# Attention blocks in pairs, q times state in four quadrants of TensorE, and y in two PSUM banks, in a gated linear attention with a squared-ReLU FFN

## The chip, the cores and the metric

The kernel runs on one core of one Trainium2 chip. The metric is the device time of one execution in microseconds (us), the median of several executions.

## The reference

Per batch and head (4 x 8, sequence 768, head size 48) a 48 x 48 state decays and is read at each token, and the result, heads side by side, goes through a feed-forward network with squared ReLU. All of it is float32 on TensorE; the two weight matrices come as float64 words and are converted on the chip.

```python
for t in range(S):
    state = alpha[:, :, t, :, None] * state + einsum('bhd,bhe->bhde', k[:, :, t], v[:, :, t])
    y[:, :, t] = einsum('bhd,bhde->bhe', q[:, :, t], state)
x = y.transpose(0, 2, 1, 3).reshape(3072, 384)
out = np.maximum(x @ w_in, 0) ** 2 @ w_out        # w_in 384 x 2048, w_out 2048 x 384
```

## The kernel before, in words

**Blocks and groups.** The sequence is cut in 6 chunks of 128 tokens. A block `n` is one chunk `c = n // 4` of one batch; there are 24. Four blocks, the four batches of a chunk, make a group of 512 tokens, and the FFN works on one group at a time while the attention of the next group is interleaved with it. The heads of a block are handled as `NP = 4` pairs `p`, with `e` = 0 or 1 for the even and the odd head of a pair; the even head lives in partitions 0 to 47, the odd one in 64 to 111.

**Steps of one attention block**, each a small function (lines of the kernel before): `aT`, `qT`, `kT` (L211) transpose alpha, q and k on TensorE; `ln` (L220, ScalarE) takes the logarithm, `sn` (L225, VectorE) the running sum in time, `eb` and `ei` (L234, L238, ScalarE) its exponential and the inverse; `mq` and `mk` (L248, VectorE) scale q and k by them into `qs` and `ks`; `sc` (L261, TensorE) forms the scores of the eight heads with the even heads on the lower and the odd ones on the upper half of the rows; `am` (L269, VectorE) copies the causal half of the scores to `am_t`, one copy for even and one for odd heads; `kr` (L279) turns `ks` back and `kc` (L284, ScalarE) copies it; `kv` (L290) multiplies it by v for the state; `sm` and `st` (L305, L356, VectorE) update the state `s_t`; `y` forms the output in PSUM, and `ev` (L345, ScalarE) copies it in 12 pieces to `xT`, the transposed input of the FFN.

**The product y** has two parts that accumulate in one PSUM bank. The first (L318) is q times state: the states of the two heads of a pair lie on the diagonal of a 128 x 128 tile that is zero elsewhere, so that one matmul does two heads, four in a block; all 128 rows and columns of TensorE are used. The second (L325) is scores times v: eight matmuls of 128 rows and 48 or 64 columns, alternating between the lower and the upper half of the columns.

**PSUM** has two pools of four banks: `ps_att` for the attention (and for every second tile of the first FFN product in groups 1 to 5), and `ps_ffn`. Tiles are given out round robin.

**Stages in time.** First the attention of blocks 0 to 3, in an order that is written out by hand. Then group 0: 16 units `ffn_in` (L425) and 32 units `ffn_out` (L498), spread over 16 slots; each slot also has one stage of attention of the next four blocks and one call of `next_weights`, which starts the load of one weight chunk, finishes the conversion of another (`convert_second`, L147 to L154, VectorE) and begins a third (`convert_first`, L130 to L140, VectorE and ScalarE). Then groups 1 to 5, each with a first product `ffn_in_pair` (L461), which has no attention beside it, and a second one, 28 units `ffn_product` (L532) of four matmuls. Beside those units the attention of the next group runs: `PLAN` (L628) gives for each step the unit at which it is issued, counted from the start of its block, and `BEGIN` (L632) the four starts, 0, 6, 12 and 18. Every unit and step issues in this one order on all engines, so each engine's queue is in the order of the plan. `sum_x` (L373, VectorE) makes sums of `xT` for the following first product. `combine` at L373 also makes sums of the hidden tiles after units 5 to 16.

**Loads** go over the SP queue; `load(n + 1)` is issued at `aT` of block `n`. The inputs a, q and k have two buffers each, v has three; `qs` and `ks` have one.

Of the kernel before, what the change touches and what calls it, by code (L numbers as in the profile page):

```python
# [15 lines left out]
GB = 4  # L16
# [7 lines left out]
def kernel(  # L24
# [46 lines left out]
    def kept(name, n, shape):  # L71
        return [consts.tile(shape, FP32, name=f"{name}{i}") for i in range(n)]

    NIN = 2
    NV = 3
    tiles = {x: kept(f"{x}_in", NIN, [128, H, 64]) for x in "aqk"}
# [1 line left out]
        for x, value in (("a", 1.0), ("q", 0.0), ("k", 0.0)):  # L78
            nc.gpsimd.memset(tiles[x][i][:, :, D:64], value)
    tiles["v"] = kept("v_in", NV, [128, H * D])  # L80
    s_t = kept("s", B, [128, NP, 128])
    for t in s_t:
        nc.gpsimd.memset(t, 0.0)

# [33 lines left out]
    half = {}  # L118
# [54 lines left out]
    am_t = kept("am", NAM, [128, 2, NP, 128])  # L173
# [120 lines left out]

    def state(n, e):
        rows = slice(64 * e, 64 * e + D)
        return rows, s_t[n % B][rows, :, 80 * e : 80 * e + D]

    def sm(n):
        if n // B in range(1, NCH - 1):  # L300
# [6 lines left out]
                )  # L307
            blk[n]["kv"] = t

    def y(n):  # L310
        v_in = tiles["v"][n % NV]

        per = NP // 2 if n == GB - 1 else NP
        ys = blk[n]["y"] = [bank(n, "y", (per, C)) for _ in range(NP // per)]

        if n // B:
            for p in range(NP):
                nc.tensor.matmul(  # L318
                    out=ys[p // per][:, p % per, :],
                    lhsT=s_t[n % B][:, p, :], rhs=blk[n]["qs"][:, p, :],  # L320
                    start=(p % per == 0), stop=False, skip_group_check=True,
                )
        for p in range(NP):
            for e in range(2):
                nc.tensor.matmul(  # L325
                    out=ys[p // per][64 * e : 64 * e + D + G * e, p % per, :],
                    lhsT=v_in[:, (2 * p + e) * D - G * e : (2 * p + e + 1) * D],
                    rhs=am_t[n % NAM][:, e, p, :],
                    start=(n // B == 0 and p % per == 0), stop=True, skip_group_check=True,
                )  # L330

    def ev(n):
        g, t = divmod(n, GB)
        if t == 0:
            xT[g] = x_pool.tile([128, KM, GB * C], FP32, tag="xT", name="xT")
        ys = blk[n].pop("y")
        per = NP // len(ys)

        for p in range(NP):
            copy = nc.vector.tensor_copy if p >= per else nc.scalar.copy  # L340
            for r, f, end in ((64, 2 * p * D + 32, 2 * (p + 1) * D), (0, 2 * p * D, (2 * p + 1) * D)):
                while f < end:
                    kk, to = divmod(f, 128)
                    m = min(end - f, *(RUN[i % 128] for i in (r, to)))
                    copy(  # L345
                        out=xT[g][to : to + m, kk, t * C : (t + 1) * C],
                        in_=ys[p // per][r : r + m, p % per, :],
                    )
                    r, f = r + m, f + m

    def st(n):
        if n // B < NCH - 1:
# [16 lines left out]
    HT, HM, NR2 = GB * C // 2, DM // 2, NJ // 4  # L369
# [144 lines left out]
    PRODUCTS = (("1", 0), ("5", 3), ("6", 1), ("7", 2), ("2", 0), ("4", 2), ("3", 3))  # L514
# [64 lines left out]
    steps = {f.__name__: f for stage in stages for f in stage}  # L579
# [14 lines left out]

    def attention(i):
        n, k = divmod(i, len(stages))
        if n < NBLK:
            for f in stages[k]:  # L600
                f(n)
            if k == 0 and n + 1 < NBLK:
                load(n + 1)

    NS = GB * len(stages)
    NG = NBLK // GB
    units = [(KM * GB * C, ffn_in, (0, j)) for j in range(NJ)]

    units += [(NJ // NW * DM, ffn_out, (0, t, i)) for i in range(NW) for t in range(GB)]
    total = sum(c for c, _, _ in units)  # L610
    done = 0
    attention(NS)
    for slot in range(NS):
        if slot < NS - 1:
            attention(NS + slot + 1)
        next_weights()
        if 0 <= slot - (NS - 3) < NR2:
            sum_w_in(slot - (NS - 3))
        if slot == NS - 1:
            sum_x(1)  # L620
        while units and done * NS < total * (slot + 1):
            c, f, args = units.pop(0)
            f(*args)
            done += c
    sum_w_in(NR2 - 1)
    NU = len(PRODUCTS) * NR2

    PLAN = (  # L628
        (0, (aT, ln, sn, eb, ei)), (2, (qT, mq, kT, mk)), (4.5, (kr, kc)), (5, (sc, am)),
        (5.5, (kv,)), (6.5, (sm, y, ev, st)),  # L630
    )
    BEGIN = (0, 6, 12, 18)  # L632
    for g in range(1, NG):

        for j in range(NJ // 2 + 1):
            for i, step in enumerate("ABacCDd"):
                if j - step.islower() in range(NJ // 2):
                    ffn_in_pair(g, j - step.islower(), step)
                if g == 1 and j < NJ // 2 and i in (1, 4):
                    sum_w_out(2 * j + i // 4)  # L640
        todo = [
            (begin + at, f, NS // len(stages) * (g + 1) + t)
            for t, begin in enumerate(BEGIN) for at, fs in PLAN for f in fs
        ]
        todo = sorted(todo, key=lambda x: x[0]) + [(NU - 3, sum_x, g + 1)]
        for u in range(NU):
            while g + 1 < NG and todo and todo[0][0] <= u:
                _, f, n = todo.pop(0)
                f(n)
                if f == aT and n + 1 < NBLK:  # L650
                    load(n + 1)
            ffn_product(g, *divmod(u, NR2))


# [28 lines left out]
```

## Time and profile before

| what | us |
|---|---|
| median of 3 runs | 616.08 |
| lowest and highest of them | 614.52, 617.27 |
| the profiled execution | 615.03 |
| its span in the profile | 613.2 |
| TensorE busy (PE) | 599.4 |
| VectorE busy (DVE) | 372.3 |
| ScalarE busy (ACT) | 245.6 |

The span runs from the first to the last instruction of the program; 1.83 us of the profiled execution lie around it. PE are the matmuls and PEld the loads of their stationary operand, which overlap them. A float32 matmul appears as two records, so a unit of four matmuls shows as x8; transposes have one record each. In a row of groups, `out<-in` names the tiles, then come the shapes, the count, busy time and the mean of one in ns, and the idle time of the engine ahead of them with what ended it. In a row of the timeline the first number is the start in us from the beginning of the span, the second the length to the end of the last instruction of the row; matmuls are pipelined, so the difference of two starts tells what a row took, not its length.

### The profile page before, as it was taken

The numbers are of one execution on the slowest core, as the hardware profiler recorded it, in microseconds if no ns is written. First come the engines' busy times: TensorE is split into PE (matmuls) and PEld (weight loads), VectorE is DVE, ScalarE is ACT, GpSimd is POOL, SyncE is SP. The second block draws the span as 40 slices with busy tenths as digits, with TensorE's granted clock in tenths as the row PEclk, the third lists the DMA queues.
The fourth block names the chain that finished last, engine by engine and source line by source line (L and its number), as shares of the span: only waits on it lengthen the run. The fifth ranks groups of instructions, "written<-read, shape, count | busy, mean of one in ns | idle before, by whom it ended". The sixth has DMA issues, their size and how long they took to land.

```text
span 613.2 us, 9325 instructions
## 1 busy us (share of the span) xinstructions
PE 599.4 (98%) x3684; PEld 516.1 (84%) x3684; DVE 372.3 (61%) x685; ACT 245.6 (40%) x613; POOL 3.8 (1%) x18
## 2 busy tenths in 40 slices
PE   7889999999999999999999999999999999999997
PEld 4755456667889999889999988999988999988997
DVE  6776858787775754565664466574456564356440
ACT  3859785532333443234333333343233244323200
POOL 2000000000000000000000000000000000000000
PEclk8979999999999999999999999999999999999999
DMA  9978375404003320403330400332130220000001
GB/s 151 255 180 188 105 152 168 91 1 104 0 1 66 52 40 27 78 1 53 53 52 13 90 2 5 61 56 36 53 52 0 53 52 2 29 25 0 1 1 51
DMA packets 108715, 36.77 MB, mean 60 GB/s; under 512 B 100480, under 2 KB 103552, under 8 KB 108672
## 3 DMA queue, kind: packets, MB, share of 16 engines
q1 hardware_dynamic: 108672, 36.18, 28.8%
q8 instruction: 29, 0.48, 0.4%
q14 instruction: 14, 0.11, 0.1%
HBM read 31.46 MB, written 4.72 MB: 59 GB/s over the span
## 4 chain that ended last, share of the span: by engine, by line
PE 87%; ACT 5%; DVE 5%; issue 1%; DMA 1%; SPq 0%; DVEq 0%
PE h L461 31%; PE o L532 31%; PE o L498 7%; PE sc L261 4%; PE y L325 3%; PE y L318 3%; PE kv L290 2%; ACT xT L345 2%; PE aT L211 1%; PE kr L279 1%; PE qT L211 1%; PE kT L211 1%; PE h L425 1%; DVE power L147 1%; ACT hid L431 1%
## 5 line engine op out<-in xcount | busy, mean ns | idle before, releaser
L461 PE MATMUL h<-xT,w_in 128*128 128x256 f32 x480 | 124.0, 379 | 0.0
L461 PEld LDWEIGHTS h<-xT,w_in 128*128 128x128 f32 x480 | 91.1, 190 | 12.4
L345 ACT COPY xT<-y 32x128 f32<-32x128 f32 (+3 forms) x282 | 72.8, 258 | 38.9 <-PE y L325 33.4
L532 PE MATMUL o<-w_out,hid 128*128 128x192 f32 x480 | 84.9, 329 | 0.0
L532 PEld LDWEIGHTS o<-w_out,hid 128*128 128x128 f32 x480 | 77.3, 190 | 1.9 <-issue 1.4
L474 DVE TENSOR_TENSOR hid<-h,u 128x256 f32<-128x256 f32 x120 | 50.9, 424 | 28.8 <-PE h L461 25.0
L479 ACT ACTIVATE hid<-hid 128x256 f32<-128x256 f32 x40 | 16.7, 417 | 114.6 <-DVE hid L474 114.6
L269 DVE COPY_PREDICATED am<-causal,sc 128x512 f32<-128x512 uint32 x48 | 32.3, 728 | 41.8 <-PE sc L261 41.8
L474 DVE TENSOR_TENSOR u<-h,u 128x256 f32<-128x256 f32 x80 | 33.9, 423 | 33.6 <-PE h L461 21.2
L225 DVE TENSOR_TENSOR_SCAN la<-again,la 128x512 f32<-128x512 f32 x24 | 29.4, 1223 | 33.3 <-ACT la L220 33.3
L461 PE MATMUL h<-s3x,ws 128*128 128x256 f32 x160 | 47.6, 379 | 0.0
L425 PE MATMUL h<-xT,w_in 128*128 128x512 f32 x96 | 43.5, 603 | 1.5 <-DVE w_in L154 1.5
L498 PE MATMUL o<-w_out,hid 128*128 128x384 f32 x128 | 42.8, 489 | 0.4 <-DVE w_out L154 0.4
L532 PE MATMUL o<-t,s 128*128 128x192 f32 x240 | 42.4, 328 | 0.0
L461 PE MATMUL h<-s3x,w_in 128*128 128x256 f32 x160 | 41.1, 379 | 0.0
L532 PEld LDWEIGHTS o<-t,s 128*128 128x128 f32 x240 | 38.9, 190 | 0.5
L498 PEld LDWEIGHTS o<-w_out,hid 128*128 128x128 f32 x128 | 23.7, 190 | 16.2 <-ACT r L430 0.6
L425 PEld LDWEIGHTS h<-xT,w_in 128*128 128x128 f32 x96 | 18.0, 194 | 21.6 <-issue 20.4
L220 ACT ACTIVATE la<-aT 128x512 f32<-128x512 f32 x24 | 14.2, 593 | 52.4 <-PE aT L211 52.3
L461 PEld LDWEIGHTS h<-s3x,w_in 128*128 128x128 f32 x160 | 30.4, 190 | 4.1
L461 PEld LDWEIGHTS h<-s3x,ws 128*128 128x128 f32 x160 | 30.4, 190 | 4.1
L261 PEld LDWEIGHTS sc<-qs,ks 48*128 48x128 f32 x384 | 23.3, 187 | 6.4 <-issue 3.3
(93 smaller groups left out, 849.6 us busy)
## 6 DMA issues: line engine op xcount, KB each, us to landing
raw<-in_moe_w_in_dram SPq DMA_DIRECT2D x8, 768.0 KB, 6.4
raw<-in_moe_w_out_dram SPq DMA_DIRECT2D x8, 768.0 KB, 4.3
a_in<-in_alpha_dram SPq DMA_DIRECT2D x24, 192.0 KB, 3.3
q_in<-in_q_dram SPq DMA_DIRECT2D x24, 192.0 KB, 4.0
k_in<-in_k_dram SPq DMA_DIRECT2D x24, 192.0 KB, 4.5
v_in<-in_v_dram SPq DMA_DIRECT2D x24, 192.0 KB, 4.3
out_dram<-osb SPq DMA_DIRECT2D x24, 192.0 KB, 2.0
```

The lines of the kernel that those rows point to most:

```text
L211: nc.tensor.transpose(out=ps[:, p, :], in_=rows[:, 128 * p : 128 * (p + 1)], identity=ident)
L225: nc.vector.tensor_tensor_scan(out=la.rearrange("a p t -> a (p t)"), data0=again.rearrange("a p t -> a (p t)"), data1=la.rearrange("a p t ...
L261: nc.tensor.matmul(out=ps[e][:, p, :], lhsT=blk[n]["ks"][rows, p, :], rhs=blk[n]["qs"][rows, p, :], start=True, stop=True,)
L269: nc.vector.copy_predicated(out=am_t[n % NAM][:, e], mask=causal.bitcast(U32).unsqueeze(1).to_broadcast([128, NP, C]), data=ps,)
L318: nc.tensor.matmul(out=ys[p // per][:, p % per, :], lhsT=s_t[n % B][:, p, :], rhs=blk[n]["qs"][:, p, :], start=(p % per == 0), stop=False, ...
L325: nc.tensor.matmul(out=ys[p // per][64 * e : 64 * e + D + G * e, p % per, :], lhsT=v_in[:, (2 * p + e) * D - G * e : (2 * p + e + 1) * D], ...
L345: copy(out=xT[g][to : to + m, kk, t * C : (t + 1) * C], in_=ys[p // per][r : r + m, p % per, :],)
L425: nc.tensor.matmul(out=ps, lhsT=w[:, kk, c0 : c0 + 128], rhs=xT[g][:, kk, :], start=(kk == 0), stop=(kk == KM - 1),)
L461: nc.tensor.matmul(out=ps, lhsT=a, rhs=b, start=(step.isupper() and i == 0), stop=(i == len(pairs) - 1), skip_group_check=True,)
L474: nc.vector.tensor_tensor(out=o, in0=ps, in1=z, op=ALU.add)
L498: nc.tensor.matmul(out=acc[t][:, 0:DM], lhsT=hid[i][:, j, t * C : (t + 1) * C], rhs=w_out[i][:, j, :], start=(i == 0 and j == 0), stop=(i ...
L532: nc.tensor.matmul(out=acc[k][:, t, :], lhsT=lhs[:, j, t * C : (t + 1) * C], rhs=rhs[:, j, :], start=(first and r + j + t == 0), stop=(r = ...
```

## The change

- The two states of a pair no longer lie on the diagonal of a 128 x 128 tile: `s_t` is [128, 4, 64], and from block 4 on q times state is one matmul per head, of 48 rows and 48 or 64 columns. With `place`, the column half is `e ^ p % 2`, so that four successive heads use four different quarters of TensorE (rows 0 or 64, columns 0 or 64).
- From block 4 on, `y` forms two blocks at once, in two banks: one for the even heads of both blocks, one for the odd. Scores times v goes to the same places, so that its column halves follow each other as 0, 1, 1, 0 and no longer 0, 1, 0, 1.
- `ev` copies two blocks with one instruction (256 instead of 128 elements per partition), 12 for a pair of blocks.
- The plan is one for a pair of blocks. Both transposes back, both score products and both `kv` stand together, and `y` of both. Group 0 uses the same plan with its times multiplied by 2.2 and pairs begun at 0 and 31 of 64 units of cost; groups 1 to 4 use it with pairs begun at 0 and 12.5 of 28 units.
- `qs` and `ks` have two buffers. a, q and k of block `n + 2` are loaded after `kT` of block `n`, v of the next two blocks after `y`.

The FFN's own products, the conversion of the weights and the attention of blocks 0 to 3 keep their operations; `y` of these blocks is only written in another way.

```diff
-    s_t = kept("s", B, [128, NP, 128])
+    s_t = kept("s", B, [128, NP, 64])
...
-        t = blk[n][f"{x}s"] = work(f"{x}s")
+        t = blk[n][f"{x}s"] = work(f"{x}s", 2)
...
-        return rows, s_t[n % B][rows, :, 80 * e : 80 * e + D]
+        return rows, s_t[n % B][rows, :, G * e : G * e + D]
...
+    def place(n, p, e):
+        if n < GB:
+            per = NP // len(blk[n]["y"])
+            return blk[n]["y"][p // per], e, lambda t: t[:, p % per]
+        return blk[n]["y"][e], e ^ p % 2, lambda t: t[:, n % 2, p // 2]
...
-            for p in range(NP):
-                nc.tensor.matmul(
-                    out=ys[p // per][:, p % per, :],
-                    lhsT=s_t[n % B][:, p, :], rhs=blk[n]["qs"][:, p, :],
...
+            ns, ys = [n, n + 1], [bank(n, "y", (2, NP // 2, C)) for _ in range(2)]
...
+        def product(m, p, e, lhsT, rhs):
+            ps, half, slot = place(m, p, e)
+            key = half, [ps is t for t in ys].index(True)
+            nc.tensor.matmul(
+                out=slot(ps)[64 * half : 64 * half + D + G * e], lhsT=lhsT, rhs=rhs,
+                start=key not in seen, stop=True, skip_group_check=True,
+            )
+            seen.add(key)
+        heads = [(m, p, e) for m in ns for p in range(NP) for e in range(2)]
...
+        for m, p, e in heads:
+            if m // B:
+                rows = slice(64 * e, 64 * e + D)
+                product(m, p, e, s_t[m % B][rows, p, 0 : D + G * e], blk[m]["qs"][rows, p, :])
+        for m, p, e in heads:
+            cols = slice((2 * p + e) * D - G * e, (2 * p + e + 1) * D)
+            product(m, p, e, tiles["v"][m % NV][:, cols], am_t[m % NAM][:, e, p, :])
...
+                    y_in = ps[r : r + m, :, p // 2] if w == 2 else slot(ps)[r : r + m]
+                    x_out = x[to : to + m, kk, t : t + w] if w == 2 else x[to : to + m, kk, t]
+                    copy(out=x_out, in_=y_in)
...
-    PLAN = (
-        (0, (aT, ln, sn, eb, ei)), (2, (qT, mq, kT, mk)), (4.5, (kr, kc)), (5, (sc, am)),
-        (5.5, (kv,)), (6.5, (sm, y, ev, st)),
-    )
-    BEGIN = (0, 6, 12, 18)
+    PLAN = (
...
+        (3.5, "aT1 ln1 sn1 eb1 ei1"),
...
+        (7.0, "kr0 kc0 kr1 kc1"),
+        (8.5, "sc0 sc1 am0 am1"),
+        (9.0, "kv0 kv1"),
+        (11.0, "sm0 y0 ev0 st0"),
+        (11.5, "sm1 st1"),
+    )
...
+    events += attention(1, (0.0, 31.0), 2.2)
...
+            events = attention(g + 1, (0.0, 12.5), 1) + [(NU - 3, sum_x, (g + 1,))]
```

More of the change, by code (lines that the diff above doesn't have):

```diff
@@ L308, in sm @@
             blk[n]["kv"] = t
-    def y(n):
[L311 to L316, printed above, removed]
-            for p in range(NP):
-                nc.tensor.matmul(
-                    out=ys[p // per][:, p % per, :],
-                    lhsT=s_t[n % B][:, p, :], rhs=blk[n]["qs"][:, p, :],
-                    start=(p % per == 0), stop=False, skip_group_check=True,
-                )
[L323 to L330, printed above, removed]
+    def place(n, p, e):
[3 more added lines that the diff above has]
+        return blk[n]["y"][e], e ^ p % 2, lambda t: t[:, n % 2, p // 2]
@@ new lines, in y @@
+    def y(n):
+        if n < GB:
+            per = NP // 2 if n == GB - 1 else NP
+            ns, ys = [n], [bank(n, "y", (per, C)) for _ in range(NP // per)]
+        else:
+            ns, ys = [n, n + 1], [bank(n, "y", (2, NP // 2, C)) for _ in range(2)]
+        seen = set()
+        def product(m, p, e, lhsT, rhs):
[7 more added lines that the diff above has]
+        heads = [(m, p, e) for m in ns for p in range(NP) for e in range(2)]
+        for m in ns:
+            blk[m]["y"] = ys
+        for m, p, e in heads:
[5 more added lines that the diff above has]
+            product(m, p, e, tiles["v"][m % NV][:, cols], am_t[m % NAM][:, e, p, :])
@@ L332, in ev @@
     def ev(n):
         g, t = divmod(n, GB)
+        w = 1 if n < GB else 2
         if t == 0:
             xT[g] = x_pool.tile([128, KM, GB * C], FP32, tag="xT", name="xT")
-        ys = blk[n].pop("y")
-        per = NP // len(ys)
+        x = xT[g].rearrange("a k (t c) -> a k t c", c=C)
         for p in range(NP):
-            copy = nc.vector.tensor_copy if p >= per else nc.scalar.copy
-            for r, f, end in ((64, 2 * p * D + 32, 2 * (p + 1) * D), (0, 2 * p * D, (2 * p + 1) * D)):
+            copy = nc.vector.tensor_copy if n == GB - 1 and p >= NP // 2 else nc.scalar.copy
+            for e, f, end in ((1, 2 * p * D + 32, 2 * (p + 1) * D), (0, 2 * p * D, (2 * p + 1) * D)):
+                ps, half, slot = place(n, p, e)
+                r = 64 * half
@@ L344, in ev @@
                     m = min(end - f, *(RUN[i % 128] for i in (r, to)))
[L345 to L348, printed above, removed]
+                    y_in = ps[r : r + m, :, p // 2] if w == 2 else slot(ps)[r : r + m]
+                    x_out = x[to : to + m, kk, t : t + w] if w == 2 else x[to : to + m, kk, t]
+                    copy(out=x_out, in_=y_in)
                     r, f = r + m, f + m
+        for m in range(n, n + w):
+            blk[m].pop("y")
     def st(n):
@@ L593 @@
         steps[f](*([int(rest[0]), rest[1:]] if f == "load" else map(int, rest)))
[L597 to L622, printed above, removed]
-            f(*args)
-            done += c
-    sum_w_in(NR2 - 1)
-    NU = len(PRODUCTS) * NR2
-    PLAN = (
-        (0, (aT, ln, sn, eb, ei)), (2, (qT, mq, kT, mk)), (4.5, (kr, kc)), (5, (sc, am)),
-        (5.5, (kv,)), (6.5, (sm, y, ev, st)),
-    )
@@ L632, with attention @@
-    BEGIN = (0, 6, 12, 18)
+    PLAN = (
+        (0.0, "aT0 ln0"),
+        (1.0, "qT0"),
+        (2, "sn0 eb0 ei0"),
+        (3.0, "mq0 kT0 mk0"),
+        (3.5, "aT1 ln1 sn1 eb1 ei1"),
+        (5.0, "qT1 kT1 mk1"),
+        (6.0, "mq1"),
+        (7.0, "kr0 kc0 kr1 kc1"),
[4 more added lines that the diff above has]
+    )
+    def attention(g, begin, scale):
+        out = []
+        for at, fs in PLAN:
+            for f in fs.split():
+                for t in begin:
+                    n = GB * g + 2 * begin.index(t) + int(f[-1])
+                    out.append((t + at * scale, steps[f[:-1]], (n,)))
+                    if f[:-1] == "kT" and n + 2 < NBLK:
+                        out.append((t + at * scale, load, (n + 2, "aqk")))
+                    if f == "y0":
+                        for m in range(n + 2, min(n + 4, NBLK)):
+                            out.append((t + at * scale, load, (m, "v")))
+        return sorted(out, key=lambda x: x[0])
@@ new lines, in weave @@
+    def weave(units, events):
+        at = 0
+        for cost, f, args in units:
+            while events and events[0][0] <= at:
+                _, e, given = events.pop(0)
+                e(*given)
+            f(*args)
+            at += cost
+        for _, e, given in events:
+            e(*given)
+    NG, NU = NBLK // GB, len(PRODUCTS) * NR2
+    units = [(2, ffn_in, (0, j)) for j in range(NJ)]
+    units += [(1, ffn_out, (0, t, i)) for i in range(NW) for t in range(GB)]
+    events = [(4 * i, next_weights, ()) for i in range(2 * NW)] + [(0, load, (GB + 1,))]
@@ L633 @@
+    events += [(52 + 4 * r, sum_w_in, (r,)) for r in range(NR2 - 1)]
+    events += attention(1, (0.0, 31.0), 2.2)
+    events += [(60, sum_x, (1,)), (61, sum_w_in, (NR2 - 1,))]
+    weave(units, sorted(events, key=lambda x: x[0]))
     for g in range(1, NG):
@@ L640 @@
                     sum_w_out(2 * j + i // 4)
[L641 to L652, printed above, removed]
+        events = []
+        if g + 1 < NG:
+            events = attention(g + 1, (0.0, 12.5), 1) + [(NU - 3, sum_x, (g + 1,))]
+        weave([(1, ffn_product, (g, *divmod(u, NR2))) for u in range(NU)], events)
 _INS = ['q', 'k', 'v', 'alpha', 'moe_w_in', 'moe_w_out']
```

## The prediction

> **What bounds the kernel now.** I read the page first, its busy time and the chain that ended last:
>
> ```profile
> span 613.2 us, 9325 instructions
> PE 599.4 (98%) x3684; PEld 516.1 (84%) x3684; DVE 372.3 (61%) x685; ACT 245.6 (40%) x613; POOL 3.8 (1%) x18
> ...
> PE 87%; ACT 5%; DVE 5%; issue 1%; DMA 1%; SPq 0%; DVEq 0%
> ```
>
> PE is busy for 98% of the span and makes 87% of the chain. An average hides stages, so the windows came next: the last part of group 0, one first FFN product, and the second product with attention beside it, in group 1 and in group 4.
>
> ```profile
> 94.00:146.26 52.26, 52.26 (x245) 33.65 (x246) 42.22 (x73) 25.01 (x50) 0.00 (x0) 1.00 0.32 81
> 146.26:184.25 37.99, 37.99 (x178) 33.40 (x178) 28.64 (x65) 12.61 (x31) 0.00 (x0) 1.00 0.17 32
> 184.25:244.75 60.50, 60.50 (x481) 58.00 (x480) 33.94 (x60) 23.67 (x68) 0.00 (x0) 1.00 0.25 47
> 479.70:534.97 55.27, 55.27 (x434) 52.57 (x432) 28.38 (x44) 21.29 (x64) 0.00 (x0) 1.00 0.18 37
> ```
>
> Columns: length, then busy time of PE, PEld, DVE, ACT, POOL, then granted clock. PE fills each window at full clock; DVE and ACT have 40% and more to spare. The waits of PE from 34 us on are only two, both in group 0, on converted weights:
>
> ```profile
> PE h L425 <- DVE w_in L154: 1.5, 1, 1.5
> PE o L498 <- DVE w_out L154: 0.4, 1, 0.4
> ```
>
> So from 34 us on the end is set by how much time PE's own stream takes. Whatever shortens that stream counts in full; what DVE or ACT save counts only in those 1.9 us.
>
> **What the stream loses today.** This is PE's timeline over one attention block of group 2:
>
> ```profile
> 191.90 0.60 PE L279 MATMUL kr<-ident,ks 128*128 128x128 f32 x4
> 192.43 1.16 PE L261 MATMUL sc<-qs,ks 48*128 48x128 f32 x16
> 193.52 1.57 PE L532 MATMUL o<-t,s 128*128 128x192 f32 x8
> 194.92 1.03 PE L290 MATMUL kv<-v_in,kc 128*128 128x96 f32 x8
> 195.79 0.60 PE L211 MATMUL aT<-ident,a_in 128*128 128x128 f32 x4
> 196.22 1.47 PE L532 MATMUL o<-t,s 128*128 128x192 f32 x8
> 197.53 1.05 PE L318 MATMUL y<-qs,s 128*128 128x128 f32 x8
> 198.51 1.09 PE L325 MATMUL y<-am,v_in 128*48 128x128 f32 x16
> 199.53 1.57 PE L532 MATMUL o<-t,s3x 128*128 128x192 f32 x8
> 200.94 0.27 PE L211 MATMUL qT<-ident,q_in 128*128 128x128 f32 x1
> ```
>
> Differences of starts give each row's time. Four transposes take 0.43 (195.79 to 196.22) but 0.53 ahead of sc; a unit of eight records takes 1.31 (196.22 to 197.53) but 1.40 and 1.41 behind sc and behind the second part of y. Inside sc and inside that part, narrow windows show six records each:
>
> ```profile
> 192.75 0.50 PE L261 MATMUL sc<-qs,ks 48*128 48x128 f32 x6
> 198.66 0.51 PE L325 MATMUL y<-am,v_in 128*48 128x128 f32 x6
> ...
> L261 PE MATMUL sc<-qs,ks 48*128 48x128 f32 x384 | 27.9, 285 | 0.0
> L325 PE MATMUL y<-am,v_in 128*48 128x128 f32 (+1 forms) x384 | 26.5, 278 | 1.4 <-ACT xT L345 1.4
> ```
>
> Less one record (285 and 278 ns), three pairs advance by two steps in 0.22 and 0.23: 0.11 us per two records. So two half-used matmuls run side by side and a pair costs what one full record of 128 columns costs (197.53 to 198.51 is 0.98 for eight, 0.88 at 0.11, the rest a change). Sixteen records are worth 0.88.
>
> From that the price of changing the array's form: sc with its neighbours takes 0.53 + 1.09 + 1.40 = 3.02, undisturbed 0.43 + 0.88 + 1.31 = 2.62: 0.40 for going in and out. For y, 0.98 + 1.02 + 1.41 = 3.41 against 0.88 + 0.88 + 1.31 = 3.07: 0.34, of which 0.20 for leaving (half of sc's 0.40) and 0.14 for going from the full form to column halves.
>
> **The change part by part.** On PE, one block's end in a second FFN product stood like this before (group 1; kr, sc, kv and y of block 9, o a unit):
>
> ```order
> L279 MATMUL kr<-ident,ks 128x128 x4
> L261 MATMUL sc<-qs,ks 128x128 x8
> L532 MATMUL o<-t_3_157,s3x 128x192 x4
> L290 MATMUL kv<-v_in_93,kc 128x96 x4
> L211 MATMUL aT<-ident,a_in_81 128x128 x4
> L532 MATMUL o<-w_out_112,hid 128x192 x4
> L318 MATMUL y<-qs,s_97 128x128 x4
> L325 MATMUL y<-am_127,v_in_93 48x128
> L325 MATMUL y<-am_127,v_in_93 64x128
> ```
>
> and stands like this now, for blocks 8 and 9 together:
>
> ```order
> L282 MATMUL kr<-ident,ks 128x128 x8
> L553 MATMUL o<-t_3_153,s3x 128x192 x4
> L553 MATMUL o<-t_0_154,s_1173 128x192 x4
> L264 MATMUL sc<-qs,ks 128x128 x16
> L293 MATMUL kv<-v_in_95,kc 128x96 x4
> L293 MATMUL kv<-v_in_93,kc 128x96 x4
> L553 MATMUL o<-t_1_155,s_1173 128x192 x4
> L553 MATMUL o<-t_2_156,s_1173 128x192 x4
> L333 MATMUL y<-qs,s_96 48x128
> L333 MATMUL y<-qs,s_96 64x128
> ```
>
> The two sc stand together, so a pair of blocks goes in and out of row halves once; q times state is 48- and 64-column matmuls, 16 for the pair.
>
> *Scores.* One of two changes of form goes: 0.40 per pair.
>
> *y.* Before, a pair costs 2 x (0.88 + 0.88 + 0.34) = 4.20. Now q times state is 32 records. The trace shows no record in a quarter of the array. Nearest are sc (row halves side by side, 0.11 per two) and scores times v (column halves side by side, 0.11 per two); both kinds of halving run at the full rate, so I take four at a time: 32 / 4 x 0.11 = 0.88. The bounds are 0.88 and 3.52 (one at a time). The Trainium skill, TensorEngine Tiling (Array Packing), Key Properties, says that different tiles can load weights and multiply in parallel; no run here shows four. Going into quarters: between 0.14 and 0.20; the loads are of 48 and 64 columns as in the second part, so 0.14. From quarters to column halves 0.14, and 0.20 for leaving. Scores times v is 32 records at two a time, 1.76. Sum 0.14 + 0.88 + 0.14 + 1.76 + 0.20 = 3.12: 1.08 less.
>
> *The order 0, 1, 1, 0 of column halves.* A half that comes twice running must end before its next begins. Two records then still overlap with the other half, only shifted. Between nothing and a tenth of 1.76; I take half, 0.09 more.
>
> Per pair 0.40 + 1.08 - 0.09 = 1.39. There are ten pairs (blocks 4 to 23, all behind another chunk): 13.9 us.
>
> *Group 0.* There conversion and attention share DVE. Before, up to the weights of the seventh unit:
>
> ```order
> L147 SCALAR_TENSOR_TENSOR power<-raw,power 128x768
> L151 SCALAR_TENSOR_TENSOR w_in_107<-upper,w_in_107 128x768
> L154 TENSOR_TENSOR w_in_107<-w_in_107,power 128x768
> L130 TENSOR_SCALAR power<-raw 128x768
> L134 TENSOR_SCALAR upper<-raw 128x768
> L225 SCALAR_TENSOR_TENSOR la<-again,la 128x512
> L147 SCALAR_TENSOR_TENSOR power<-raw,power 128x768
> ```
>
> Now the scans stand elsewhere:
>
> ```order
> L228 SCALAR_TENSOR_TENSOR la<-again,la 128x512
> L251 TENSOR_TENSOR qs<-qT,b 128x512
> L251 TENSOR_TENSOR ks<-kT,inv 128x512
> L228 SCALAR_TENSOR_TENSOR la<-again,la 128x512
> L150 SCALAR_TENSOR_TENSOR power<-raw,power 128x768
> L154 SCALAR_TENSOR_TENSOR w_in_107<-upper,w_in_107 128x768
> L157 TENSOR_TENSOR w_in_107<-w_in_107,power 128x768
> ```
>
> Before, a scan that waits for ACT stood ahead of the conversion of w_in_108 (that is the 1.5 us wait); now two stand ahead of that of w_in_107. One wait goes, one of its kind comes. I take nothing for the sum, with bounds of -1.9 (both waits go) and +2.9, a whole conversion late:
>
> ```profile
> L147 DVE SCALAR_TENSOR_TENSOR power<-raw,power 128x768 uint32<-128x768 uint32 x16 | 15.2, 949 | 0.2
> ...
> L154 DVE TENSOR_TENSOR w_in<-w_in,power 128x768 f32<-128x768 f32 x8 | 7.7, 958 | 0.3
> L151 DVE SCALAR_TENSOR_TENSOR w_in<-upper,w_in 128x768 f32<-128x768 uint32 x8 | 7.6, 951 | 0.0
> ```
>
> *Edits at nothing.* Copies of y, loads and the memset:
>
> ```profile
> L345 ACT COPY xT<-y 32x128 f32<-32x128 f32 (+3 forms) x282 | 72.8, 258 | 38.9 <-PE y L325 33.4
> L466 ACT COPY u<-h 128x256 f32<-128x256 f32 x40 | 14.4, 359 | 13.7 <-PE h L461 13.7
> 530.91 3.33 ACT L345 COPY xT<-y 32x128 f32<-32x128 f32 x12 [8.25 <-PE y L325]
> 534.81 0.59 PE L461 MATMUL h<-xT,w_in 128*128 128x256 f32 x2
> k_in<-in_k_dram SPq DMA_DIRECT2D x24, 192.0 KB, 4.5
> v_in<-in_v_dram SPq DMA_DIRECT2D x24, 192.0 KB, 4.3
> L83 POOL MEMSET s<- 128x512 f32 x4 | 1.9, 528 | 0.0
> L269 DVE COPY_PREDICATED am<-causal,sc 128x512 f32<-128x512 uint32 x48 | 32.3, 728 | 41.8 <-PE sc L261 41.8
> L373 DVE TENSOR_TENSOR s<-s,hid 128x512 f32<-128x512 f32 x15 | 10.3, 686 | 15.8 <-PE o L532 15.8
> ```
>
> A pair's copies take about 12 x 0.36 = 4.3 instead of 6.2, on ACT, which PE does not wait for. At a group's end they lie between y and the next first product: before, 3.33 fit into 3.9 (530.91 to 534.81, three units); now 4.3 fit into four units, 5.2. Without that cover each of four ends would cost up to 4.3. A pair's a, q and k are loaded after kT, at unit 3 or 5, and needed at 12.5 and later: over seven units, 9 us, against 4.5 to land, and three loads in a row still fit. SP's loads of v wait for y and, at a group's end, behind stores; kv needs v only after the next first product, 38 us on. The memset gets shorter at the start, where PE waits for other things; bounds 0 and half of 1.9.
>
> *New waits.* kv now stands right behind sc and takes banks that am has to empty. The first am can begin when the first sc ends; the second sc hides 0.88 of it, and one am takes 0.73, so the first kv, 0.87 long, finds its bank free and the second nearly so. Behind am on DVE stand the combines and sm, which PE does not need for two units. I take 0; one combine (0.69) ahead of am would cost PE about that much.
>
> The sum: the profiled execution took 615.03 (span 613.2 and 1.83 around it) and would take 615.03 - 13.9 = 601.1. The median of the runs is 1.05 above it: 616.08 - 13.9 = **602.2**.
>
> **Rivals.**
>
> *Two at a time.* Quarters that share rows do not run beside each other. Then q times state is 16 x 0.11 = 1.76 per pair, 0.88 more, 8.8 over ten: 611.0. For it: no record in the trace has four. Against it: column halves that share all 128 rows do run side by side. The Trainium skill, TensorE: Matmul & The Clock Gate, section What overlaps and what doesn't, states a rule that gives this case: a weight load overlaps a running matmul only when their row groups differ. The trace does not bear it out for y, where 16 loads share all rows and a pair still takes 0.11.
>
> *DVE is late.* A combine or a conversion stands ahead of am, and kv waits 0.69 in each of the eight pairs of groups 2 to 5: 5.5, so 607.7. For it: the two steps now stand together. Against it: DVE is busy 33.94 of 60.50.
>
> *One at a time, slower.* Each change of quarter empties the array. Then 32 x 0.11 = 3.52 per pair, 2.64 more, 26.4 over ten: 628.6. It decides from 0.88 + 1.39 = 2.27 per pair on, 0.07 per record. Against it: sc changes row halves at every record at the full rate. The Trainium skill, TensorEngine Tiling (Array Packing), Key Properties, lays the drain on a change of mode and not on one of tile, and sc agrees.
>
> **How the numbers follow.** Forecast 0.72, DVE late 0.11, two at a time 0.12, one at a time 0.05. The forecast's own range is 599 (both waits gone, no price for the order: 602.2 - 2.8) to 605 (a conversion late). With late DVE on top, to 609, 83 in 100 are held, so the range is 599 to 609. A measurement of this kernel tells about 0.5% (3 us) from no change: faster means under 613.0. Forecast and late DVE are, and two at a time unless waits come on top (0.05 for that): faster 0.90, same 0.05, slower 0.05.
>
> **What would show it.** In the changed profile: q times state of a pair should take 0.9 to 1.0 from its first record to scores times v (1.8 would be two at a time, 3.5 one); scores times v 1.8 to 1.9; the pair of sc 1.97; a second product with attention 60.50 - 2.8 = 57.7 (55.27 - 2.8 = 52.5 in group 4); no waits of PE after 150 us; a wait on w_in in group 0 of 1 to 2. The prediction fails if those stages keep 60.5, or if PE waits for am.

## The result, and the profile after

The changed kernel takes 598.86 us (median of 4 runs, 598.62 to 600.51), beside 616.67 of the kernel before (4 runs, 614.52 to 617.73): the ratio is 0.972, with a 95% interval of 0.969 to 0.975. The forecast was 602.2 in a range of 599 to 609; the sign came as forecast, the fall is larger, and the median lies 0.14 below the low end of the range. The same kernel in a second set of runs took 599.66 (598.69 to 601.02) beside 615.01 before, ratio 0.974 (0.971 to 0.977), so the fall is some 15 to 18 us where 13.9 were forecast.

The profiled execution took 598.62. Its page gives:

```profile
span 596.8 us, 9525 instructions
PE 584.5 (98%) x3844; PEld 503.5 (84%) x3844; DVE 370.6 (62%) x685; ACT 223.8 (37%) x493; POOL 3.0 (0%) x18
...
PE 96%; ACT 2%; DVE 1%; issue 0%; DVEq 0%
```

PE has 160 records more (32 instead of 16 in each of ten pairs) and still 14.9 us less work; it makes 96% of the chain instead of 87%. It waits once after 36 us, ahead of its first FFN record, on a converted weight:

```profile
36.53 6.62 PE L446 MATMUL h<-xT,w_in 128*128 128x512 f32 x12 [0.33 <-DVE w_in L157]
```

This is PE's timeline over one pair of blocks, in the same second product as the one block shown of before (the product is that of group 1, the attention beside it that of group 2):

```profile
191.04 1.04 PE L282 MATMUL kr<-ident,ks 128*128 128x128 f32 x8
191.92 1.47 PE L553 MATMUL o<-t,s3x 128*128 128x192 f32 x8
193.22 1.46 PE L553 MATMUL o<-t,s 128*128 128x192 f32 x8
194.61 2.06 PE L264 MATMUL sc<-qs,ks 48*128 48x128 f32 x32
196.60 2.02 PE L293 MATMUL kv<-v_in,kc 128*128 128x96 f32 x16
198.46 2.79 PE L553 MATMUL o<-t,s 128*128 128x192 f32 x16
201.18 1.10 PE L333 MATMUL y<-qs,s 48*48 48x128 f32 x32
202.22 1.97 PE L333 MATMUL y<-am,v_in 128*48 128x128 f32 x32
204.11 1.08 PE L553 MATMUL o<-t,s3x 128*128 128x192 f32 x5
```

Read from start to start: the two score products take 1.99, q times state 1.04 for 32 records, scores times v 1.89. No row carries a wait. Some 0.16 of the 1.04 do not grow with the records (the run with quarters alone, below, takes 0.60 for 16 of them, so 16 more take 0.44). That leaves 0.88 for 32 records: four run at a time, a round of four every 0.11.

For the stages I measure the second product with attention from its first `o` to the first `h` of the next product. (The prediction's windows began 0.27 earlier and ended 0.17 later, so its 60.50 is 60.06 here, and the 57.7 that it forecast is 57.3; an expectation that gives 57.6 for the changed kernel counts so too.) Groups 1 and 4 before, in the columns of the prediction's windows:

```profile
184.52:244.58 60.06, 60.06 (x478) 57.56 (x477) 33.65 (x60) 23.67 (x68) 0.00 (x0) 1.00 0.26 47
479.98:534.81 54.83, 54.83 (x431) 52.13 (x430) 28.10 (x44) 21.29 (x64) 0.00 (x0) 1.00 0.18 37
```

and, after, the same two stages:

```profile
179.75:236.92 57.17, 57.17 (x510) 55.10 (x509) 33.34 (x60) 19.38 (x44) 0.00 (x0) 1.00 0.32 63
466.55:518.39 51.84, 51.84 (x462) 49.81 (x461) 27.83 (x44) 17.26 (x40) 0.00 (x0) 1.00 0.19 39
```

The first product of group 1 did not move (38.42 before, from 146.10 to 184.52, and 38.43 after, from 141.32 to 179.75). Each stage with attention lost 2.89 in groups 1 to 3 and 2.99 in group 4, two pairs each, and PE fills it wholly at full clock in both kernels. Of the span's 16.4, the four stages make 3 x 2.89 + 2.99 = 11.7. The other 4.8 lie ahead of the first product: group 0 (first `h` to its end) went from 146.10 - 37.72 = 108.4 to 141.32 - 36.53 = 104.8, and the first `h` came 1.2 earlier, mostly because `qT` and `kT` of a block, which stood ahead of it (36.01 to 37.72 before), now stand behind it.

### The profile page after: what moved, and what is told of

It reads as the page before. It is cut to its first block, busy times and chain, and to the rows that moved or that the text cites. A ratio compares the mean times of both kernels' runs of the same rounds, so it can differ in the third digit from the quotient of the medians.

```text
span 596.8 us, 9525 instructions
## 1 busy us (share of the span) xinstructions
PE 584.5 (98%) x3844; PEld 503.5 (84%) x3844; DVE 370.6 (62%) x685; ACT 223.8 (37%) x493; POOL 3.0 (0%) x18
## 4 chain that ended last, share of the span: by engine, by line
PE 96%; ACT 2%; DVE 1%; issue 0%; DVEq 0%
PE h L482 32%; PE o L553 31%; PE h L446 7%; PE o L519 7%; PE y L333 5%; PE sc L264 4%; PE kv L293 3%; PE aT L214 2%; PE kT L214 2%; PE qT L214 2%; PE kr L282 2%; ACT xT L367 1%; PE warm L192 1%; DVE ks L251 0%; DVE la L228 0%
## 5 line engine op out<-in xcount | busy, mean ns | idle before, releaser
L482 PEld LDWEIGHTS h<-xT,w_in 128*128 128x128 f32 x480 | 91.1, 190 | 12.4
L367 ACT COPY xT<-y 32x256 f32<-32x256 f32 (+3 forms) x162 | 52.6, 337 | 100.7 <-PE y L333 98.0
L553 PE MATMUL o<-w_out,hid 128*128 128x192 f32 x480 | 83.6, 326 | 0.0
L272 DVE COPY_PREDICATED am<-causal,sc 128x512 f32<-128x512 uint32 x48 | 31.1, 725 | 28.8 <-PE sc L264 28.8
L519 PEld LDWEIGHTS o<-w_out,hid 128*128 128x128 f32 x128 | 23.6, 190 | 14.9 <-issue 0.2
L553 PE MATMUL o<-t,hid 128*128 128x192 f32 x160 | 28.5, 329 | 0.0
L502 DVE SCALAR_TENSOR_TENSOR hid<-hid 128x512 f32<-128x512 f32 x40 | 27.2, 681 | 0.0
```

The source lines that it names most:

```text
L272: nc.vector.copy_predicated(out=am_t[n % NAM][:, e], mask=causal.bitcast(U32).unsqueeze(1).to_broadcast([128, NP, C]), data=ps,)
L367: copy(out=x_out, in_=y_in)
L482: nc.tensor.matmul(out=ps, lhsT=a, rhs=b, start=(step.isupper() and i == 0), stop=(i == len(pairs) - 1), skip_group_check=True,)
L502: nc.vector.scalar_tensor_tensor(out=h2, in0=h2, scalar=0.0, in1=h2, op0=ALU.max, op1=ALU.mult)
L519: nc.tensor.matmul(out=acc[t][:, 0:DM], lhsT=hid[i][:, j, t * C : (t + 1) * C], rhs=w_out[i][:, j, :], start=(i == 0 and j == 0), stop=(i ...
L553: nc.tensor.matmul(out=acc[k][:, t, :], lhsT=lhs[:, j, t * C : (t + 1) * C], rhs=rhs[:, j, :], start=(first and r + j + t == 0), stop=(r = ...
```

## The experiments

Each was timed beside the kernel before on the same chip, and the ratios are to that. Since PE's stream sets the time of every stage after group 0, the stage of group 1 (60.06 before, 57.17 after) shows an edit's cost much more finely than the time does, and the readings below rest on it.

### The state as one tile again

The two states go back to the diagonal of a 128 x 128 tile, q times state to one full matmul per pair of heads. All else stays in pairs of blocks. (To make room for the larger state, `b` has two buffers instead of three and `sm` uses one of `la`.)

```diff
-    s_t = kept("s", B, [128, NP, 64])
+    s_t = kept("s", B, [128, NP, 128])
...
-        return blk[n]["y"][e], e ^ p % 2, lambda t: t[:, n % 2, p // 2]
+        return blk[n]["y"][p // 2], e, lambda t: t[:, n % 2, p % 2]
...
+                nc.tensor.matmul(
+                    out=slot(ps), lhsT=s_t[m % B][:, p, :], rhs=blk[m]["qs"][:, p, :],
+                    start=first, stop=False, skip_group_check=True,
+                )
```

> The changed kernel with q times state in the full form again (one matmul of 128 rows and columns for a pair of heads, states on the diagonal); pairs of blocks, y of two blocks in two banks, plan and copies stay. (To make room, the sum in the state update uses another tile and one buffer less is kept of the decays.) Quarters theory: 16 full records of 0.11 instead of 32 records at 0.027, and one change of form less: 1.79 - 0.90 - 0.13 = 0.76 per pair more, 7.6 over ten, so about 606.5; a second product with attention 57.6 + 1.5 = 59.1. Rival (the gain is the pairing, the quarters give nothing): 599.

It took 609.98, ratio 0.989 (0.985 to 0.993). The window of its stage, and its `y` of a pair on PE:

```profile
186.54:245.21 58.67, 58.67 (x478) 57.18 (x477) 33.35 (x60) 19.78 (x44) 0.00 (x0) 1.00 0.31 62
```

```profile
205.25 2.79 PE L559 MATMUL o<-t,s 128*128 128x192 f32 x16
207.88 1.95 PE L346 MATMUL y<-qs,s 128*128 128x128 f32 x16
209.76 1.97 PE L333 MATMUL y<-am,v_in 128*48 128x128 f32 x32
211.65 1.57 PE L559 MATMUL o<-t,s3x 128*128 128x192 f32 x8
```

Sixteen full records take 1.88 where 32 quarter records take 1.04, which is 0.84 more. The two units ahead of them take 2.63 (205.25 to 207.88), where ahead of quarters they take 2.72 (198.46 to 201.18), which is 0.09 less. That makes 0.75 per pair, 0.76 were expected, and the stage is 1.50 longer than after. The rival, that quarters give nothing, falls. Scores times v takes 1.89 in both. The time itself rose by more than the stages (606.5 were expected), since this kernel also starts later: ahead of its first `h` PE waits 4.6 for `kc`, where the changed kernel waits 1.7, and that `h` comes at 41.53. Whether the buffers did that was not tried; that part says nothing on quarters.

### Quarters alone

The other way round: the kernel before, with its plan of single blocks, its loads and copies, but with the new state, `place` and `product`, two banks for one block.

```diff
-    s_t = kept("s", B, [128, NP, 128])
+    s_t = kept("s", B, [128, NP, 64])
...
+            ns, ys = [n], [bank(n, "y", (NP // 2, C)) for _ in range(2)]
```

> The kernel before, one block at a time and with its old plan, with q times state in quarters alone (y of a block in two half-filled banks, even and odd heads). Sum of the prediction: per block 0.88 - 0.44 for the product, less 0.14 for going into quarters: 0.30, 6.0 over twenty blocks, about 610.5 where the kernel before takes 616.5; a second product with attention 60.06 - 1.2 = 58.9. Rival (the extra bank of a block makes PE wait in a pool of four): no gain or slower, with waits of PE in those stages.

It took 609.22, ratio 0.990 (0.987 to 0.994). Its stage, and `y` of one block:

```profile
183.50:242.39 58.89, 58.89 (x510) 55.24 (x509) 33.70 (x60) 22.93 (x68) 0.00 (x0) 1.00 0.25 48
```

```profile
195.21 1.47 PE L550 MATMUL o<-t,s 128*128 128x192 f32 x8
196.60 0.67 PE L330 MATMUL y<-qs,s 48*48 48x128 f32 x16
197.20 1.09 PE L330 MATMUL y<-am,v_in 128*48 128x128 f32 x16
198.22 1.57 PE L550 MATMUL o<-t,s3x 128*128 128x192 f32 x8
```

PE has no wait in these stages, so the second bank of a block costs nothing. The stage loses 1.17, that is 0.29 per block; the prediction's terms give 0.88 + 0.14 - (0.14 + 0.44 + 0.14) = 0.30. Everything but the quarters (the run above) loses 60.06 - 58.67 = 1.39. The two add up to 2.56, and together the change brings 2.89, because in pairs the way into quarters and out of them is paid once for two blocks. It costs 0.16 in its own row (0.60 from start to start, less 0.44) and 0.08 on the unit ahead (1.39, from 195.21 to 196.60, where 1.31 is undisturbed); the full form, taken in pairs, saves 0.08 of its own (2 x 0.98 - 1.88). That leaves 0.16 per pair, 0.32 for the two pairs of a stage. Twenty blocks at 0.29 are 5.9, and the medians differ by 615.01 - 609.22 = 5.8.

### The scores apart

```diff
-        (8.5, "sc0 sc1 am0 am1"),
-        (9.0, "kv0 kv1"),
+        (8.5, "sc0 am0"),
+        (9.5, "sc1 am1 kv0 kv1"),
```

> The changed kernel with the scores of the two blocks of a pair one unit apart, so that the array goes into row halves and out of them twice per pair. Form-change theory: 0.40 per pair more, 4.0 over ten, about 603; a second product with attention 57.6 + 0.8 = 58.4. Rival (a change of form costs nothing that other work does not fill): 599.

It took 603.74, ratio 0.979 (0.975 to 0.983). Its stage, and the scores of a pair:

```profile
182.51:240.47 57.96, 57.96 (x510) 55.19 (x509) 33.52 (x60) 19.41 (x44) 0.00 (x0) 1.00 0.32 62
```

```profile
197.37 1.16 PE L264 MATMUL sc<-qs,ks 48*128 48x128 f32 x16
198.47 1.57 PE L553 MATMUL o<-t,s 128*128 128x192 f32 x8
199.96 1.16 PE L264 MATMUL sc<-qs,ks 48*128 48x128 f32 x16
```

The stage is 0.79 longer than after, 0.395 per pair. One way into row halves and out again costs 0.40, as the prediction had worked out from rows of before.

### The order of the heads in q times state

Three kernels change only the order in which the 16 matmuls of a pair's q times state are issued. The first alternates between two quarters for eight records, then between the other two, for one block and then the other. The second does so for both blocks together, so that two quarters get 16 records before the others get any. The third fills one quarter with eight records after another.

```diff
-        for m, p, e in heads:
+        for m, p, e in sorted(heads, key=lambda h: (h[0], h[1] % 2)):   # two quarters
+        for m, p, e in sorted(heads, key=lambda h: h[1] % 2):           # halves in turn
+        for m, p, e in sorted(heads, key=lambda h: (h[2], h[1] % 2)):   # one quarter
```

> The changed kernel with the 16 q-times-state matmuls of a pair in another order: eight that use only two quarters in turn, rows 0 with columns 0 and rows 64 with columns 64 or the other two, four of a block and then four. The work and the places of the results are the same. If only neighbours in the queue overlap: two at a time, 1.76 instead of 0.88 per pair, 8.8 over ten, about 607.5. Rival (each quarter takes its own work from the queue, whatever the order): 599.

> The same matmuls sorted by quarter: four in the first, four in the second and so on. If only neighbours overlap: one at a time but for the seams, 29 or more records of 0.11 in a row, about 3.2 to 3.5 instead of 0.88 per pair, 23 to 26 over ten, 622 to 625, slower than the kernel before. Rival (each quarter takes its own work): 599.

> The changed kernel with the sixteen q-times-state matmuls of a pair ordered so that the first eight, of both blocks, use two quarters and the last eight the other two: eight records per quarter in a row, where the order of four earlier (e2) had four. From the one-quarter order (e3), in which a quarter's first five records ran alone and its last three beside the next quarter's: a quarter holds three records ahead, so 8 + 8 - 3 = 13 steps of 0.11 instead of 8, 0.53 per pair more, a second product with attention 57.17 + 1.06 = 58.2, about 604.5. Rivals: unlimited queues per quarter, 57.2 and 599.5; neighbours alone, 16 steps, 58.9 and 607.5.

Two quarters for a block took 600.34, ratio 0.974 (0.971 to 0.978), which the time does not tell from after. Its stage, 0.10 longer than after, and its pair:

```profile
183.30:240.57 57.27, 57.27 (x510) 55.20 (x509) 33.33 (x60) 19.40 (x44) 0.00 (x0) 1.00 0.33 63
```

```profile
204.73 1.15 PE L333 MATMUL y<-qs,s 48*48 48x128 f32 x32
205.82 1.97 PE L333 MATMUL y<-am,v_in 128*48 128x128 f32 x32
```

So it is not that a matmul can overlap only with its neighbours in the queue: two quarters in turn still run four at a time (1.09). My theory of neighbours fell. One quarter after another took 612.88, ratio 0.997 (0.995 to 0.999). Its stage, and its pair:

```profile
186.07:246.12 60.05, 60.05 (x510) 57.97 (x509) 33.33 (x60) 19.40 (x44) 0.00 (x0) 1.00 0.31 60
```

```profile
207.51 2.54 PE L333 MATMUL y<-qs,s 48*48 48x128 f32 x32
209.98 1.97 PE L333 MATMUL y<-am,v_in 128*48 128x128 f32 x32
```

The order alone costs all that the change brought. Yet 2.47 is neither what one at a time would take, 32 x 0.11 = 3.5, nor 1.04: both theories on record missed. The narrow windows show why; even heads have records of 48*48, odd heads, all queued behind them, of 48*64. The first row is of the timeline from 207.50 to 207.98; the others are groups by form (count, busy us and mean ns of one) from two windows of this kernel, 208.46 to 208.48 and 208.80 to 208.84.

```profile
207.51 0.63 PE L333 MATMUL y<-qs,s 48*48 48x128 f32 x4
...
L333 PE MATMUL y<-qs,s 48*48 48x128 f32 x5 | 0.5, 269 | 0.0
L333 PE MATMUL y<-qs,s 48*64 48x128 f32 x1 | 0.3, 320 | 0.0
...
L333 PE MATMUL y<-qs,s 48*48 48x128 f32 x3 | 0.5, 269 | 0.0
L333 PE MATMUL y<-qs,s 48*64 48x128 f32 x2 | 0.4, 269 | 0.0
```

At first one quarter works alone, a record every 0.12 (four in 0.63, the last 0.27 long, make three steps). By 208.48 the first record of an odd head is running, and at 208.80 three of the even heads still are, 269 ns long, hence begun after 208.53. So a later matmul for a free quarter begins before earlier ones for a busy quarter: each quarter takes its own work, and the queue lets it run ahead by a few records. If the next quarter begins x rounds after the one before, three seams and eight rounds make 8 + 3x; with 0.17 that does not grow with the records (1.04 less eight rounds of 0.109) 2.30 are left, 21.1 rounds: x = 4.4. That is 0.48, or four steps of 0.12: the next quarter begins with the fifth record of the one before it, when three are still to come. These are the three that the windows show.

The halves in turn were made to test that number, on a seam that comes once. The expectation counted five rounds ahead of the seam, 13 in all, and a stage of 58.2; with the 4.4 it is 12.4 rounds, 1.35, and 1.52 with the 0.17. It took 603.54, ratio 0.982 (0.979 to 0.986):

```profile
180.81:238.95 58.14, 58.14 (x510) 56.06 (x509) 33.33 (x60) 19.40 (x44) 0.00 (x0) 1.00 0.32 62
```

```profile
202.24 1.59 PE L333 MATMUL y<-qs,s 48*48 48x128 f32 x32
203.76 1.97 PE L333 MATMUL y<-am,v_in 128*48 128x128 f32 x32
```

The pair takes 1.52, the stage 0.97 more than after. Here two quarters have work waiting at the seam, three records each. Were three all that may wait in both together, the seam would come 1.5 rounds later and the pair would take 1.68; so the three are counted for each quarter. In the first kernel of the three a quarter gets four records at a time, one at work and three that may wait, and only 0.05 per pair is lost.

### Copies one block at a time

```diff
-                    copy(out=x_out, in_=y_in)
+                    for i in range(w):
+                        y_in = ps[r : r + m, i, p // 2] if w == 2 else slot(ps)[r : r + m]
+                        copy(out=x[to : to + m, kk, t + i], in_=y_in)
```

> The changed kernel with y copied one block at a time, 24 copies of 128 elements for a pair instead of 12 of 256: about 6.5 us of ACT instead of 4.0. Theory (ACT is covered, but at a group's end four units, 5.2 us, hide the copies): at most 1.3 at each of four ends and nothing elsewhere, 599 to 605; if the first matmuls of the next product need only the first third of the copies, nothing, 599 to 600. Rival (the larger copies are part of the gain): 603 or more, with waits spread over the stages.

It took 599.61, ratio 0.974 (0.971 to 0.977), the same as the unaltered change beside it. The copies of the last pair of group 4 after, and the next product behind them:

```profile
513.22 4.37 ACT L367 COPY xT<-y 32x256 f32<-32x256 f32 x12 [9.84 <-PE y L333]
518.39 0.59 PE L482 MATMUL h<-xT,w_in 128*128 128x256 f32 x2
```

and with single copies:

```profile
515.14 5.04 ACT L367 COPY xT<-y 32x128 f32<-32x128 f32 x24 [9.84 <-PE y L333]
520.33 0.59 PE L482 MATMUL h<-xT,w_in 128*128 128x256 f32 x2
```

The copies end 0.80 ahead of the product after, and 0.15 ahead with single copies. The four units cover both, and PE waits for neither.

### The plan of group 0, and the change again

The first three steps of the pair's plan are pulled together to its start for group 0 and the second pair begins at 26, so that the running sums on VectorE stand ahead of other conversions than before. The unaltered changed kernel ran beside it.

```diff
+    PLAN0 = ((0.0, "aT0 ln0 sn0 eb0 ei0"), (1.0, "qT0")) + PLAN[3:]
...
-    events += attention(1, (0.0, 31.0), 2.2)
+    events += attention(1, (0.0, 26.0), 2.2)
```

> The changed kernel with another plan in group 0 alone: the scan and the exponentials of a pair's first block stand right behind its logarithm, and the second pair begins at 26 instead of 31, right behind the copies of y of the first. Theory (in the old order a scan stood ahead of a conversion and waited for a logarithm that was itself behind copies and squares on ACT; the new order parted them): waits of PE on w_in or w_out come back, 0.5 to 2 in all, group 0 longer by that, 0.5 to 2 us slower than the changed kernel run beside it. Rival (what group 0 gained beyond two pairs comes from fewer copies on ACT): no new waits, same time.

> The changed kernel once more, unaltered, to stand on the same chip beside the others and to show how far the first 40 us differ from run to run (first FFN record at 36.5 in the first profile, 37.6 to 38.7 in later kernels that leave that part alone). 599 to 600; second products with attention 57.17 again, to 0.05.

It took 601.06, ratio 0.977 (0.973 to 0.980), the unaltered one 599.66, ratio 0.974 (0.971 to 0.977): the intervals overlap, and the time does not tell them apart. The trace does, on PE's waits. With the other plan:

```profile
37.80 7.55 PE L446 MATMUL h<-xT,w_in 128*128 128x512 f32 x12 [0.97 <-DVE w_in L157]
58.33 5.39 PE L446 MATMUL h<-xT,w_in 128*128 128x512 f32 x12 [0.49 <-DVE w_in L157]
93.51 1.53 PE L519 MATMUL o<-w_out,hid 128*128 128x384 f32 x4 [0.38 <-DVE w_out L157]
```

and with the plan as it is, in the second set of runs:

```profile
37.64 7.71 PE L446 MATMUL h<-xT,w_in 128*128 128x512 f32 x12 [1.27 <-DVE w_in L157]
```

With the other plan, waits within group 0 on both weights are there, as in the kernel before (1.48 and 0.37); with the plan of the change none is left behind the first unit. So the plan, which sets what stands ahead of the conversions on VectorE, decides whether those waits come; whether the scans or the earlier second pair did it was not parted. Group 0 took 144.59 - 37.80 = 106.8, and 143.29 - 37.64 = 105.7 unaltered; of the difference 0.87 are the two waits behind the first unit. The stage of group 1 took 57.18 unaltered, as in the first set.

## Why the prediction was right, step by step

**Four at a time.** Forecast 0.9 to 1.0 for q times state of a pair, measured 1.04 after. The rival of two at a time wanted 1.8, that of one at a time 3.5, and neither occurred. The rule for the first, that a weight load overlaps a running matmul only in other rows (the Trainium skill, TensorE: Matmul & The Clock Gate, What overlaps and what doesn't), does not hold here: two of the four quarters share their rows in every round of 0.109. That only a change of mode drains the array, not one of tile (the Trainium skill, TensorEngine Tiling (Array Packing), Key Properties), agrees with the same row. The forecast rested on two kinds of halves that each ran at the full rate; this carried over to quarters, but, as the orders show, only as long as no quarter gets more than some four records in a row.

**Changes of form.** The 0.40 for the scores came as 0.395 (the scores apart), the gain of quarters for a single block, 0.30, as 0.29. With what the changes put on the units beside it, 0.10 ahead (2.72 for two units of 1.31) and 0.10 behind (1.41 for one, as before), `y` of a pair is 204.11 - 201.18 + 0.20 = 3.13, forecast 3.12 without the order. How the sum splits is not as forecast: going into quarters shows as this 0.10 on the unit ahead, not as 0.14.

**The order 0, 1, 1, 0.** This term was wrong: I took 0.09 per pair between nothing and 0.18, and it is nothing. Six records of scores times v in a narrow window after:

```profile
202.80 0.51 PE L333 MATMUL y<-am,v_in 128*48 128x128 f32 x6
```

Less one record this is again 0.11 per two, and the whole takes 1.89 with either order (the state as one tile has 0, 1, 0, 1). The forecast thought that a half which comes twice running holds up the other a little. The orders show of quarters that the other goes ahead meanwhile; that halves do the same is argued from the equal 1.89. Ten pairs at 0.09 are 0.9 of the miss. The other terms were 0.035 per pair too hopeful (1.39 + 0.09 = 1.48 without the order), so that the measured 1.445 per pair stands against 1.39, and ten make 14.5 against 13.9.

**Group 0.** Beyond its two pairs I took nothing, on the ground that one wait goes and one of its kind comes. Both waits of before went, and a new one on the first unit came, 0.33 in the profiled execution, 1.27 in the second set and about 0.8 with single copies. So the waits fell by 1.5 and 0.6 in the two executions, inside the bound of 1.9. (The prediction also read that DVE has 40% and more to spare. That holds beside the second products; in the last part of group 0 it was busy for 42.22 of 52.26, in the first product for 28.64 of 37.99.)

The new wait lies ahead of the first `h`, so inside group 0 PE is busy throughout after (104.79 and 105.65), and for 106.53 of the 108.38 before: its own work became 1.74 and 0.88 shorter. Two things hide more. The eight transposes `qT` and `kT` that moved behind the first `h` add 0.86. And the granted clock is half at the start of group 0, for a different time in each execution (before, after, and the second set):

```profile
37.72:38.97 1.25, 1.25 (x3) 0.67 (x3) 0.36 (x1) 1.23 (x3) 0.00 (x0) 0.50 1.05 221
36.53:39.02 2.49, 2.49 (x3) 1.14 (x4) 2.41 (x6) 1.73 (x2) 0.00 (x0) 0.50 0.99 324
37.64:42.31 4.67, 4.67 (x6) 2.09 (x7) 4.56 (x8) 1.73 (x2) 0.00 (x0) 0.50 1.23 258
```

Records of `h` follow each other in 0.86 there and in 0.43 behind it, so half of each stretch is lost: 0.62, 1.25 and 2.33. With both, the work of group 0 became 1.74 + 0.86 + 0.63 = 3.2 and 0.88 + 0.86 + 1.71 = 3.5 shorter, where two pairs at 1.445 make 2.9; the rest was not traced.

**What is left of the miss.** The profiled execution was to take 601.1; the two executions of the changed kernel took 598.62 and 600.55. In the first one the stretch at half clock lies as it did before the change (from 32.2 to 39.0), and the span's 16.4 are 11.7 in the four stages, 1.5 of waits and 3.2 in group 0, where the forecast had 11.1, nothing and 2.8. In the second one it comes 3.3 later, from 35.5 to 42.3, and group 0 is 0.9 longer; another 1.1 is lost before (the first four transposes take 0.85, from 5.56, where in the first execution they take 0.43, from 5.23). The stages behind group 0 take the same in both. Over all these kernels but the one with the larger state the first `h` came between 36.5 and 38.7. So the start varies by more than the terms that I weighed there. The forecast's own range allowed for 2.8 below; 3.3 were needed in the first set. Its high end of 609 is not what its terms give (a conversion late and late DVE make 605.1 + 5.5 = 610.6); neither came.

**VectorE late.** It did not come: PE has no wait behind group 0's first unit, and kv follows the scores without one.

**The copies, loads and the memset** cost nothing, as forecast; for the copies the experiment on them shows the cover, which has 0.80 left.

## What to carry to other kernels

Matmuls that use a quarter of the array each ran four at a time here when successive ones went to different quarters, or when no quarter got more than four records in a row; with eight in a row a stage lost 0.97 of its 2.89 (two quarters in turn) or all of it (one after another). Put work of one array form together: here one way in and out costs 0.3 to 0.4, so that pairing blocks earned somewhat more than the quarters alone did (1.39 and 1.17 per stage). Where one engine fills its stages, read an edit from the length of a stage (here good to 0.1 us), and let the start, which varied by 2 us, not decide.

## What the runs showed of the hardware that was not expected

Each quarter of TensorE's array took its own work from the queue. It began a later matmul while earlier ones waited for another quarter, and three records of a quarter could wait so. Four quarters in turn, two in turn for eight records, two in turn for sixteen, and one for eight gave stages of 57.17, 57.27, 58.14 and 60.05. The Trainium skill, TensorE: Matmul & The Clock Gate, What overlaps and what doesn't, says that matmuls start and end strictly in program order; between quarters, the records of even and odd heads at 208.46 to 208.84 show that starts do not.
